# A recurrence and a gated feed-forward on one core: output copies of two superblocks on ScalarE, and another written-out order of the later steps

## The chip, the cores and the metric

The kernel runs on one core of a Trainium2 chip. A core has five engines, each with its own queue of instructions that it works off in order: PE (TensorE, matmuls; PEld is its weight load), DVE (VectorE), ACT (ScalarE), POOL (GpSimd) and SP (SyncE, which here only issues DMAs). They wait for each other by semaphores. The metric is the device time of one execution in microseconds (us); the median of several runs counts.

## The reference

Inputs r, k, v, w are float32 of shape (4 batches, 8 heads, 768 tokens, 48); u is (8, 48). For every batch and head a 48x48 state is carried along the tokens, and its output feeds a gated feed-forward over the 8 x 48 = 384 channels:

```python
for t in range(S):
    cur = einsum('bhd,bhe->bhde', u * k[t], v[t])
    y[t] = einsum('bhd,bhde->bhe', r[t], state + cur)
    state = w[t][..., None] * state + einsum('bhd,bhe->bhde', k[t], v[t])
x = y.transpose(0, 2, 1, 3).reshape(3072, 384)
xn = x / sqrt(mean(x * x, -1) + 1e-6) * rms_g
g, val = xn @ w_gate, xn @ w_val          # 384 -> 1536
out = (g * sigmoid(g) * val) @ w_out      # 1536 -> 384, float32
```

## The kernel before

The 768 tokens are cut into six superblocks n = 0..5 of 128 tokens; a superblock holds the same 128 tokens of the four batches j = 0..3, so 512 rows. A step is written name.n.j. Within a superblock the recurrence is done in chunk form, per (n, j):

- load_w, load_k, load_r, load_v (L208 to L237) bring 128 x 384 float32 each, all issued on SP. Eight buffers hold r, k and v each, and four pairs hold w.
- ln (ACT) takes logarithms of w; cs_mm (PE) makes cumulated sums in the PSUM pools ps_a and ps_b; for n of 3 to 5 cs_add (DVE) derives the second sum from the first; exp_r and exp_k (ACT) exponentiate in place, so exp_r comes after cs_add has read.
- r_mul and k_mul (DVE) scale r and k; w_tot (DVE) keeps the total decay. rk_tr transposes both, by PE and ACT (with rk_pe) for n below 2, by a DMA transpose issued on SP from n = 2 on.
- q_mm (PE) makes the 128x128 score blocks in two ps_q banks; q_mask_e (DVE, L465) copies the even heads with the mask; q_copy_o (ACT, L469) copies the odd ones, which q_mask_o (POOL, L476) then masks. q_mm.4.2 does j = 2 and 3 at once.
- st_mm (PE) makes the update of the state from k and cast_v's bf16 v (POOL from n = 2 on), st_new (DVE) applies it; y_mm (PE) makes the output of the recurrence.
- bonus_mul (POOL, two multiplications, L423 and L424, needs r and k), bonus_sum (DVE), bonus_v (POOL, needs v) make the term with u; x_add (DVE) adds it.
- x_sq (ACT), x_rstd (POOL, L524 and L525) and xn_mul (ACT) normalize; xn_pe (PE) with xn_out (DVE), or for n of 4 and 5 a DMA transpose xn_tr with xn_gain (DVE), bring xn to the layout of the feed-forward.

The feed-forward of a superblock runs over 12 units f of 128 of the 1536 channels: gate_mm and val_mm (PE, L566, three matmuls of 128x512 each, into ps_a and ps_b with two banks each), silu (ACT, L198), h_mul (DVE, L584). Then o_mm (PE, L629, twelve matmuls of 128x384) makes the output of 128 rows in a ps_q bank, o_out (L636 on DVE or L638 on ACT) copies it to one of three buffers ob, and out_dma (SP, L644) stores it. The pool ps_q has four banks for rk_pe, q_mm, st_mm, y_mm, xn_pe and o_mm together, so each of these on PE waits until the bank used four allocations earlier has been read.

Logarithm and exponential are in one ACT table, silu in another; every change of table is a load (L196) in ACT's queue. It falls ten times.

The order of everything is written out by hand in one string, ORDER (L25 to L126): the loop at its end (L647 to L650) calls the steps one by one, and each engine gets its instructions in just this order. The feed-forward of superblock n is woven with the recurrence of n + 1, and o_mm of n with the start of n + 2. What sets time is therefore where a step stands in each queue. OUT_DVE (L190) lists the (n, j) whose output copy goes to DVE; all others go to ACT.

Of the kernel before, what the change touches and what calls it, by code (L numbers as in the profile page):

```python
# [680 lines left out]
```

## Time and profile before

| what | value |
|---|---|
| median of 5 runs | 209.52 us (207.79 to 214.32) |
| profiled execution: its time, its span | 208.85 us, 207.1 us |
| PE, DVE, ACT, POOL busy | 190.2, 159.5, 138.7, 108.3 us |
| HBM read, written | 25.96 MB, 4.72 MB |
| output copies on DVE (L636), ACT (L638), full size | 12 of 554 ns, 11 of 480 ns |
| silu (L198), h_mul (L584) | 72 of 598 ns, 72 of 688 ns |
| one 128x384 load, issue to landing | 3.8 to 4.2 us (median by tensor) |

A page of the profile has the busy time of each engine, the span in 40 slices (each digit tenths of a slice), the groups of instructions with their busy time, the mean of one, and the idle time ahead of them. "A <- B: 0.8, 2, 0.4" in a list of waits means that A stood idle for B: 0.8 us in total, twice, 0.4 at the longest. In a timeline a line has the start, the duration, the engine, the line of the code, and in brackets the idle time ahead of it with what ended it. Busy time of PE counts matmuls in the pipeline.

### The profile page before, as it was taken

To read this page: it belongs to the slowest core of one execution; us is meant where nothing else is said; L and a number is where in the kernel's file an instruction comes from. 1 tells how busy PE (TensorE), PEld (TensorE's weight loads), DVE (VectorE), ACT (ScalarE), POOL (GpSimd) and SP (SyncE) were. 2 spreads that over 40 slices of the span, in tenths; PEclk is the share of its full clock that TensorE was granted. 3 is DMA by queue.
4 is the path that set the end of the run, shared out by engine and by line. 5 is a ranking of instruction groups with operands and counts; after the bars stand their busy time and mean duration, and the time that the engine had idled before them with its cause. 6 is when DMAs were issued, how large, how long until landed. Compare 5 with 4: busy or idle time off the path is not lost.

```text
span 207.1 us, 4352 instructions
## 1 busy us (share of the span) xinstructions
PE 190.2 (92%) x1507; PEld 111.7 (54%) x1524; DVE 159.5 (77%) x323; ACT 138.7 (67%) x282; POOL 108.3 (52%) x167
## 2 busy tenths in 40 slices
PE   5685869899999999998999999999999999999993
...
DMA  6999999999999899899899989997157110201032
GB/s 133 211 200 199 185 201 201 198 174 227 184 199 233 163 194 220 167 234 198 172 203 205 233 174 216 149 231 169 39 145 211 41 38 3 76 0 40 0 119 76
DMA packets 125727, 32.41 MB, mean 156 GB/s; under 512 B 120580, under 2 KB 124552, under 8 KB 125704
## 3 DMA queue, kind: packets, MB, share of 16 engines
...
HBM read 25.96 MB, written 4.72 MB: 148 GB/s over the span
## 4 chain that ended last, share of the span: by engine, by line
PE 52%; SPq 20%; POOL 8%; DMA 8%; ACT 4%; issue 4%; DVE 2%; POOLq 0%; DVEq 0%; ACTq 0%
SPq L211 16%; PE ps_a L566 16%; PE ps_b L566 15%; PE ps_q L629 14%; DMA rt<-in_r_dram 5%; SPq L228 4%; DMA wt<-in_w_dram 3%; POOL ruk L423 2%; POOL ruk L424 2%; PE ps_q L458 2%; PE ps_q L503 1%; POOL qts L476 1%; POOL ydiag L433 1%; PE ps_q L506 1%; PE ps_a L378 1%
## 5 line engine op out<-in xcount | busy, mean ns | idle before, releaser
L198 ACT ACTIVATE sg<-ps_a 128x512 bf16<-128x512 f32 x72 | 42.9, 598 | 32.0 <-PE ps_a L566 30.2
L584 DVE TENSOR_TENSOR ht<-ps_b,sg 128x512 bf16<-128x512 f32 x72 | 49.0, 688 | 19.3 <-PE ps_b L566 12.9
L566 PE MATMUL ps_a<-xnt,wg_sb 128*128 128x512 bf16 x207 | 58.6, 382 | 1.8 <-DMA wg_sb<-in_moe_w_gate_dram 1.0
L566 PE MATMUL ps_b<-xnt,wv_sb 128*128 128x512 bf16 x208 | 58.2, 382 | 0.3
L629 PE MATMUL ps_q<-wo_sb,ht 128*128 128x384 bf16 (+1 forms) x300 | 50.1, 319 | 0.0
L629 PEld LDWEIGHTS <-ht 128*128 128x128 bf16 x300 | 27.9, 98 | 16.5 <-DMA wo_sb<-in_moe_w_out_dram 0.2
L423 POOL TENSOR_TENSOR ruk<-rt,kt 128x384 f32<-128x384 f32 x24 | 24.6, 1024 | 23.1 <-DMA rt<-in_r_dram 17.4
L566 PEld LDWEIGHTS <-wv_sb 128*128 128x128 bf16 x216 | 23.6, 115 | 20.5 <-issue 1.5
L566 PEld LDWEIGHTS <-wg_sb 128*128 128x128 bf16 x216 | 23.2, 114 | 20.9 <-issue 1.2
L424 POOL TENSOR_TENSOR ruk<-ruk,u_bc 128x384 f32<-128x384 f32 x24 | 24.0, 999 | 1.9
L476 POOL TENSOR_SCALAR_AFFINE_SELECT qts<-qts 128x512 bf16<-128x512 bf16 x20 | 12.7, 634 | 14.3 <-ACT qts L469 14.3
L433 POOL TENSOR_TENSOR ydiag<-vt,diag 128x384 f32<-128x384 f32 x24 | 19.8, 829 | 0.4 <-DVE diag L428 0.4
L465 DVE TENSOR_TENSOR qts<-ps_q,mask_lt 128x512 bf16<-128x512 f32 x24 | 16.4, 683 | 2.4 <-PE ps_q L460 2.0
L529 ACT ACTIVATE xn<-xb,rstd 128x384 bf16<-128x384 f32 x24 | 14.4, 609 | 2.1 <-POOL rstd L525 1.9
L198 ACT ACTIVATE lw<-wt 128x384 bf16<-128x384 f32 x24 | 12.1, 517 | 5.1 <-DMA wt<-in_w_dram 5.0
L469 ACT CAST qts<-ps_q 128x512 bf16<-128x512 f32 x20 | 11.7, 583 | 4.5 <-PE ps_q L460 4.5
L511 DVE TENSOR_TENSOR xb<-ps_q,ydiag 128x384 f32<-128x384 f32 x24 | 13.2, 552 | 1.8 <-POOL ruk L424 0.9
L636 DVE COPY ob<-ps_q 128x384 f32<-128x384 f32 (+1 forms) x13 | 7.0, 539 | 9.3 <-PE ps_q L629 8.5
L196 ACT ACT_TABLE_LOAD x10 | 12.8, 1283 | 1.8 <-PEq L665 1.6
L516 ACT ACTIVATE junk<-xb 128x384 bf16<-128x384 f32 x24 | 12.4, 519 | 1.6 <-DVE xb L511 1.2
L417 DVE TENSOR_TENSOR rk<-kt,ps_b 128x384 bf16<-128x384 f32 x20 | 11.0, 549 | 2.5 <-ACT ps_b L198 2.2
L428 DVE TENSOR_REDUCE diag<-ruk 128x8 f32<-128x384 f32 x24 | 12.9, 543 | 0.0
...
## 6 DMA issues: line engine op xcount, KB each, us to landing
...
```

Source lines behind the costliest of these rows:

```text
L198: return nc.scalar.activation(**kw).ins
L211: dmas["load_" + which, n, j] = nc.sync.dma_start(out=inp[which, n, j], in_=t[j, :, n * L:(n + 1) * L, :].rearrange("h t d -> t h d")).ins
L423: nc.gpsimd.tensor_tensor(out=ruk[n, j], in0=inp["r", n, j], in1=inp["k", n, j], op=ALU.mult)
L424: nc.gpsimd.tensor_tensor(out=ruk[n, j], in0=ruk[n, j], in1=u_bc, op=ALU.mult)
L433: nc.gpsimd.tensor_tensor(out=ydiag[n, j], in0=inp["v", n, j], in1=diag[n, j].to_broadcast([128, H, D]), op=ALU.mult)
L465: nc.vector.tensor_tensor(out=qts[n, j][:, 0], in0=bank["q", n, j][0], in1=bc_mid(mask_lt, NP), op=ALU.mult)
L476: nc.gpsimd.affine_select(out=qts[n, j][:, 1], in_=qts[n, j][:, 1], compare_op=ALU.is_gt, fill=0.0, base=0, pattern=[[0, NP], [1, 128]], c ...
L511: nc.vector.tensor_tensor(out=xb[n, j], in0=bank.pop(("y", n, j)), in1=ydiag[n, j].rearrange("p h d -> p (h d)"), op=ALU.add)
L529: nc.scalar.activation(out=xn, in_=xb[n, j], func=AF.Copy, scale=rstd[n, j][:, 1:2])
L566: nc.tensor.matmul(ps, lhsT=units(ws, c, f), rhs=xnt[n][:, c, :], start=(c == 0), stop=(c == KC - 1))
L584: nc.vector.tensor_tensor(out=ht[n][:, f, :], in0=bank.pop(("v", n, f)), in1=bank.pop(("sg", n, f)), op=ALU.mult)
L629: nc.tensor.matmul(ps[:, cols], lhsT=ht[n][:, f, b * L:(b + 1) * L], rhs=wo_sb[:, f, cols], start=(f == 0), stop=(f == FC - 1))
```

## The change

Two edits. OUT_DVE loses 20, 22, 30 and 32: the output copies o_out.2.0, o_out.2.2, o_out.3.0 and o_out.3.2 go from DVE to ACT, so that all eight of superblocks 2 and 3 are on ACT. And ORDER is another permutation of the same 1063 steps from its 178th step on (its first sixteen lines are the same): of PE's 284 steps 80 stand in another place of its queue, of SP's 145 transfers 73, of POOL's 111 steps 71, of ACT's steps 150 and of DVE's 184, for these two partly because of the four copies. No step is added or left out, and no buffer count changes.

The diff, cut to the stretches that are spoken of:

```diff
--- before
+++ after
...
-load_r.1.2 silu.0.4 bonus_sum.1.0 gate_mm.0.5 bonus_mul.1.1 k_mul.1.1 q_mm.1.0 load_r.1.3 silu.0.5 val_mm.0.5
-h_mul.0.4 cast_v.1.0 load_w.2.0 q_mask_e.1.0 gate_mm.0.6 q_copy_o.1.0 load_wo.2.0 h_mul.0.5 rk_pe.1.1 load_r.2.0
-st_mm.1.0 k_mul.1.2 val_mm.0.6 load_wo.1.0 rk_tr.1.1 k_mul.1.3 gate_mm.0.7 bonus_mul.1.2 silu.0.6 r_mul.1.2 val_mm.0.7
-silu.0.7 h_mul.0.6 gate_mm.0.8 cast_v.1.1 load_w.2.1 st_new.1.0 rk_pe.1.2 bonus_v.1.0 val_mm.0.8 rk_tr.1.2 q_mm.1.1
-h_mul.0.7 q_mask_o.1.0 gate_mm.0.9 silu.0.8 r_mul.1.3 load_wo.0.0 q_copy_o.1.1 val_mm.0.9 bonus_sum.1.1 silu.0.9
-rk_pe.1.3 h_mul.0.8 bonus_v.1.1 st_mm.1.1 gate_mm.0.10 rk_tr.1.3 q_mask_e.1.1 bonus_mul.1.3 load_v.1.2 val_mm.0.10
+load_r.1.2 silu.0.4 bonus_sum.1.0 gate_mm.0.5 bonus_mul.1.1 cast_v.1.0 k_mul.1.1 val_mm.0.5 load_r.1.3 silu.0.5
+h_mul.0.4 st_mm.1.0 rk_pe.1.1 load_w.2.0 st_new.1.0 gate_mm.0.6 load_wo.2.0 load_v.1.2 val_mm.0.6 silu.0.6 h_mul.0.5
+load_wo.0.0 gate_mm.0.7 rk_tr.1.1 h_mul.0.6 q_mm.1.0 bonus_mul.1.2 r_mul.1.2 cast_v.1.1 val_mm.0.7 silu.0.7 k_mul.1.2
+gate_mm.0.8 q_copy_o.1.0 load_w.2.1 bonus_sum.1.1 val_mm.0.8 silu.0.8 h_mul.0.7 load_wo.1.0 gate_mm.0.9 q_mask_e.1.0
+q_mask_o.1.0 rk_pe.1.2 silu.0.9 r_mul.1.3 val_mm.0.9 bonus_mul.1.3 rk_tr.1.2 k_mul.1.3 q_mm.1.1 gate_mm.0.10 h_mul.0.8
+q_copy_o.1.1 rk_pe.1.3 q_mask_e.1.1 bonus_v.1.0 st_mm.1.1 load_k.2.0 val_mm.0.10 h_mul.0.9 rk_tr.1.3 q_mask_o.1.1
...
-out_dma.0.2 o_mm.1.0 bonus_mul.3.2 bonus_sum.3.1 x_sq.2.1 st_new.2.3 load_k.4.0 ln.3.1 xn_mul.2.0 out_dma.0.3
-cs_mm.3.0 x_add.2.2 cs_mm.3.1 ln.3.2 x_rstd.2.1 y_mm.2.3 cs_add.3.0 x_sq.2.2 o_mm.1.1 o_out.1.0 exp_k.3.0 x_rstd.2.2
-cs_add.3.1 exp_r.3.0 out_dma.1.0 k_mul.3.0 exp_k.3.1 load_r.4.0 bonus_v.2.3 r_mul.3.0 exp_r.3.1 xn_mul.2.1 xn_pe.2.0
-k_mul.3.1 bonus_mul.3.3 o_mm.1.2 rk_tr.3.0 x_add.2.3 xn_mul.2.2 r_mul.3.1 ln.3.3 o_out.1.1 xn_out.2.0 rk_tr.3.1
-x_sq.2.3 w_tot.3.0 w_tot.3.1 xn_pe.2.1 cs_mm.3.2 o_out.1.2 x_rstd.2.3 xn_pe.2.2 cs_mm.3.3 cs_add.3.2 load_k.4.1
-o_mm.1.3 xn_out.2.1 bonus_v.3.0 exp_r.3.2 load_v.3.1 cs_add.3.3 xn_mul.2.3 cast_v.3.0 xn_out.2.2 load_w.4.0 exp_r.3.3
-w_tot.3.2 exp_k.3.2 r_mul.3.2 xn_pe.2.3 q_mm.3.0 o_out.1.3 xn_out.2.3 load_k.4.2 exp_k.3.3 st_mm.3.0 k_mul.3.2
+o_mm.1.0 bonus_v.2.3 xn_mul.2.0 load_r.4.0 x_add.2.1 q_mask_o.2.3 ln.3.1 out_dma.0.3 x_add.2.2 x_sq.2.1 cs_mm.3.0
+bonus_sum.3.1 cs_mm.3.1 ln.3.2 load_k.4.0 x_rstd.2.1 o_mm.1.1 cs_add.3.0 x_sq.2.2 cs_add.3.1 exp_r.3.0 load_k.4.1
+bonus_mul.3.3 o_out.1.0 exp_k.3.0 r_mul.3.0 exp_r.3.1 k_mul.3.0 xn_mul.2.1 y_mm.2.3 xn_pe.2.0 r_mul.3.1 o_out.1.1
+o_mm.1.2 rk_tr.3.0 exp_k.3.1 x_add.2.3 x_rstd.2.2 ln.3.3 k_mul.3.1 x_sq.2.3 out_dma.1.0 xn_out.2.0 xn_mul.2.2
+x_rstd.2.3 w_tot.3.0 load_v.3.1 w_tot.3.1 xn_pe.2.1 cs_mm.3.2 o_out.1.2 cs_mm.3.3 bonus_mul.4.0 xn_pe.2.2 xn_out.2.1
+xn_mul.2.3 rk_tr.3.1 o_mm.1.3 cs_add.3.2 xn_out.2.2 exp_r.3.2 load_r.4.1 cs_add.3.3 exp_k.3.2 r_mul.3.2 load_r.4.2
+cast_v.3.0 xn_pe.2.3 q_mm.3.0 o_out.1.3 w_tot.3.2 bonus_v.3.0 xn_out.2.3 exp_r.3.3 st_mm.3.0 k_mul.3.2 load_v.3.2
+exp_k.3.3 gate_mm.2.0 r_mul.3.3 q_copy_o.3.0 val_mm.2.0 w_tot.3.3 load_v.3.3 k_mul.3.3 silu.2.0 gate_mm.2.1
...
-bonus_v.3.2 h_mul.2.7 gate_mm.2.9 bonus_sum.4.1 out_dma.1.1 q_mm.3.2 cast_v.3.3 silu.2.9 h_mul.2.8 val_mm.2.9
-bonus_mul.4.3 x_sq.3.0 load_k.5.0 q_mask_e.3.2 gate_mm.2.10 h_mul.2.9 val_mm.2.10 load_w.4.2 silu.2.10 bonus_sum.4.2
-gate_mm.2.11 out_dma.1.2 q_copy_o.3.2 bonus_v.3.3 h_mul.2.10 st_mm.3.3 val_mm.2.11 load_w.4.3 silu.2.11 q_mask_o.3.2
-st_new.3.3 ln.4.0 y_mm.3.1 x_rstd.3.0 out_dma.1.3 q_mm.3.3 load_r.5.1 h_mul.2.11 y_mm.3.2 bonus_v.4.0 x_add.3.1 ln.4.1
-cs_mm.4.0 bonus_v.4.1 q_mask_e.3.3 q_copy_o.3.3 o_mm.2.0 cs_add.4.0 x_sq.3.1 bonus_v.4.2 x_add.3.2 exp_k.4.0
-bonus_sum.4.3 q_mask_o.3.3 x_sq.3.2 k_mul.4.0 cs_mm.4.1 x_rstd.3.1 exp_r.4.0 o_mm.2.1 ln.4.2 cs_add.4.1 bonus_mul.5.0
-xn_mul.3.0 r_mul.4.0 exp_r.4.1 o_out.2.0 rk_tr.4.0 xn_mul.3.1 r_mul.4.1 xn_pe.3.0 exp_k.4.1 y_mm.3.3 o_out.2.1
-o_mm.2.2 k_mul.4.1 out_dma.2.0 x_rstd.3.2 x_add.3.3 rk_tr.4.1 xn_out.3.0 x_sq.3.3 w_tot.4.0 w_tot.4.1 xn_mul.3.2
-x_rstd.3.3 cs_mm.4.2 load_v.4.3 o_out.2.2 xn_pe.3.1 xn_pe.3.2 o_mm.2.3 load_k.5.1 cs_add.4.2 cast_v.4.0 xn_mul.3.3
-xn_out.3.1 exp_r.4.2 load_k.5.2 xn_out.3.2 exp_k.4.2 ln.4.3 r_mul.4.2 load_r.5.2 xn_pe.3.3 k_mul.4.2 cs_mm.4.3
-o_out.2.3 q_mm.4.0 xn_out.3.3 st_mm.4.0 load_k.5.3 w_tot.4.2 q_copy_o.4.0 cs_add.4.3 gate_mm.3.0 q_mask_e.4.0
-q_mask_o.4.0 exp_r.4.3 load_r.5.3 val_mm.3.0 exp_k.4.3 bonus_sum.5.0 bonus_mul.5.1 silu.3.0 q_mm.4.1 r_mul.4.3
+silu.2.7 st_mm.3.2 bonus_sum.4.0 gate_mm.2.8 st_new.3.2 load_w.4.1 bonus_mul.4.3 val_mm.2.8 silu.2.8 y_mm.3.0
+out_dma.1.3 h_mul.2.7 gate_mm.2.9 load_w.4.2 h_mul.2.8 q_mm.3.2 silu.2.9 bonus_v.3.1 val_mm.2.9 bonus_sum.4.1
+load_k.5.1 q_copy_o.3.2 q_mask_e.3.2 cast_v.3.3 gate_mm.2.10 load_r.5.1 x_add.3.0 bonus_v.3.2 val_mm.2.10 silu.2.10
+load_v.4.0 h_mul.2.9 q_mask_o.3.2 gate_mm.2.11 x_sq.3.0 h_mul.2.10 load_r.5.2 bonus_mul.5.0 st_mm.3.3 val_mm.2.11
+silu.2.11 st_new.3.3 ln.4.0 load_w.4.3 y_mm.3.1 y_mm.3.2 h_mul.2.11 q_mm.3.3 x_rstd.3.0 x_add.3.1 ln.4.1 cs_mm.4.0
+bonus_v.3.3 x_sq.3.1 o_mm.2.0 cs_add.4.0 x_add.3.2 x_rstd.3.1 exp_r.4.0 q_mask_e.3.3 q_copy_o.3.3 ln.4.2 bonus_sum.4.2
+q_mask_o.3.3 cs_mm.4.1 x_sq.3.2 o_mm.2.1 cs_add.4.1 exp_k.4.0 x_rstd.3.2 w_tot.4.0 r_mul.4.0 xn_mul.3.0 k_mul.4.0
+exp_r.4.1 bonus_mul.5.1 o_out.2.0 bonus_sum.4.3 rk_tr.4.0 xn_pe.3.0 xn_mul.3.1 y_mm.3.3 r_mul.4.1 cs_mm.4.2 exp_k.4.1
+x_add.3.3 o_mm.2.2 xn_mul.3.2 out_dma.2.0 k_mul.4.1 bonus_v.4.0 o_out.2.1 cs_add.4.2 rk_tr.4.1 x_sq.3.3 xn_out.3.0
+exp_k.4.2 x_rstd.3.3 bonus_sum.5.0 xn_pe.3.1 exp_r.4.2 xn_pe.3.2 o_mm.2.3 xn_out.3.1 load_k.5.2 cast_v.4.0 xn_mul.3.3
+r_mul.4.2 load_v.4.1 o_out.2.2 w_tot.4.1 xn_out.3.2 ln.4.3 load_r.5.3 k_mul.4.2 xn_pe.3.3 w_tot.4.2 cs_mm.4.3
+o_out.2.3 xn_out.3.3 q_mm.4.0 load_k.5.3 st_mm.4.0 cs_add.4.3 q_copy_o.4.0 gate_mm.3.0 q_mask_e.4.0 out_dma.2.1
+exp_k.4.3 q_mask_o.4.0 val_mm.3.0 exp_r.4.3 silu.3.0 bonus_mul.5.2 q_mm.4.1 load_v.4.2 r_mul.4.3 y_mm.4.0 w_tot.4.3
...
-val_mm.3.3 h_mul.3.2 silu.3.3 bonus_mul.5.3 gate_mm.3.4 x_sq.4.0 h_mul.3.3 load_v.5.1 val_mm.3.4 silu.3.4 load_v.5.2
-st_mm.4.1 gate_mm.3.5 h_mul.3.4 x_rstd.4.0 out_dma.2.2 val_mm.3.5 st_new.4.1 silu.3.5 cast_v.4.2 load_v.5.3
-gate_mm.3.6 xn_mul.4.0 q_mask_o.4.1 h_mul.3.5 val_mm.3.6 cast_v.4.3 load_w.5.0 silu.3.6 bonus_sum.5.1 bonus_v.4.3
-gate_mm.3.7 load_w.5.1 q_mask_e.4.1 val_mm.3.7 bonus_sum.5.2 load_w.5.2 q_mm.4.2 h_mul.3.6 xn_tr.4.0 gate_mm.3.8
-q_copy_o.4.2 q_mask_e.4.2 val_mm.3.8 silu.3.7 q_mask_o.4.2 q_copy_o.4.3 out_dma.2.3 y_mm.4.1 h_mul.3.7 silu.3.8
-y_mm.4.2 load_w.5.3 x_add.4.1 gate_mm.3.9 x_add.4.2 x_sq.4.1 val_mm.3.9 h_mul.3.8 x_sq.4.2 x_rstd.4.1 gate_mm.3.10
-q_mask_e.4.3 silu.3.9 x_rstd.4.2 val_mm.3.10 xn_mul.4.1 h_mul.3.9 silu.3.10 gate_mm.3.11 xn_tr.4.1 q_mask_o.4.3
-bonus_sum.5.3 h_mul.3.10 val_mm.3.11 cast_v.5.0 silu.3.11 cast_v.5.1 st_mm.4.2 xn_mul.4.2 y_mm.4.3 h_mul.3.11
-bonus_v.5.0 st_mm.4.3 ln.5.0 xn_tr.4.2 x_add.4.3 o_mm.3.0 cast_v.5.2 st_new.4.2 x_sq.4.3 st_new.4.3 ln.5.1 x_rstd.4.3
-cs_mm.5.0 ln.5.2 cs_mm.5.1 o_mm.3.1 cs_add.5.0 cast_v.5.3 xn_mul.4.3 cs_add.5.1 bonus_v.5.1 exp_r.5.0 xn_tr.4.3
-exp_k.5.0 r_mul.5.0 bonus_v.5.2 exp_k.5.1 k_mul.5.0 ln.5.3 cs_mm.5.2 o_mm.3.2 exp_r.5.1 rk_tr.5.0 cs_add.5.2 k_mul.5.1
-exp_r.5.2 r_mul.5.1 exp_k.5.2 r_mul.5.2 rk_tr.5.1 cs_mm.5.3 o_out.3.1 o_out.3.0 o_mm.3.3 cs_add.5.3 xn_gain.4.0
-out_dma.3.0 exp_k.5.3 xn_gain.4.1 xn_gain.4.2 exp_r.5.3 k_mul.5.2 gate_mm.4.0 r_mul.5.3 rk_tr.5.2 o_out.3.2 val_mm.4.0
-silu.4.0 k_mul.5.3 gate_mm.4.1 rk_tr.5.3 q_mm.5.0 val_mm.4.1 q_mask_e.5.0 q_copy_o.5.0 out_dma.3.1 gate_mm.4.2
+load_w.5.0 h_mul.3.2 silu.3.3 gate_mm.3.4 x_rstd.4.0 q_mask_e.4.1 val_mm.3.4 load_v.5.0 h_mul.3.3 bonus_v.4.2 silu.3.4
+st_mm.4.1 xn_mul.4.0 gate_mm.3.5 load_v.5.1 bonus_mul.5.3 st_new.4.1 y_mm.4.1 silu.3.5 val_mm.3.5 load_w.5.1 x_add.4.1
+gate_mm.3.6 h_mul.3.4 out_dma.2.2 x_sq.4.1 bonus_v.4.3 q_mm.4.2 h_mul.3.5 load_w.5.2 val_mm.3.6 q_copy_o.4.2
+q_mask_e.4.2 gate_mm.3.7 q_copy_o.4.3 q_mask_e.4.3 q_mask_o.4.2 load_v.5.2 silu.3.6 val_mm.3.7 cast_v.4.2 load_v.5.3
+silu.3.7 h_mul.3.6 x_rstd.4.1 gate_mm.3.8 xn_tr.4.0 bonus_sum.5.1 val_mm.3.8 bonus_v.5.0 xn_mul.4.1 h_mul.3.7 y_mm.4.2
+silu.3.8 load_w.5.3 cast_v.4.3 gate_mm.3.9 x_add.4.2 q_mask_o.4.3 xn_tr.4.1 val_mm.3.9 h_mul.3.8 x_sq.4.2 bonus_v.5.1
+gate_mm.3.10 silu.3.9 out_dma.2.3 x_rstd.4.2 val_mm.3.10 h_mul.3.9 silu.3.10 cast_v.5.0 gate_mm.3.11 xn_mul.4.2
+h_mul.3.10 cast_v.5.1 val_mm.3.11 xn_tr.4.2 bonus_sum.5.2 silu.3.11 y_mm.4.3 ln.5.0 bonus_v.5.2 h_mul.3.11 st_mm.4.2
+st_mm.4.3 x_add.4.3 cast_v.5.2 o_mm.3.0 st_new.4.2 cast_v.5.3 x_sq.4.3 ln.5.1 x_rstd.4.3 st_new.4.3 ln.5.2 cs_mm.5.0
+o_out.3.0 cs_mm.5.1 o_mm.3.1 xn_mul.4.3 cs_add.5.0 cs_add.5.1 xn_tr.4.3 exp_r.5.0 exp_k.5.0 r_mul.5.0 ln.5.3 k_mul.5.0
+out_dma.3.0 cs_mm.5.2 exp_r.5.1 o_mm.3.2 exp_k.5.1 cs_add.5.2 rk_tr.5.0 r_mul.5.1 exp_r.5.2 k_mul.5.1 exp_k.5.2
+o_out.3.1 r_mul.5.2 rk_tr.5.1 cs_mm.5.3 o_mm.3.3 cs_add.5.3 xn_gain.4.0 exp_r.5.3 xn_gain.4.1 xn_gain.4.2 exp_k.5.3
+bonus_sum.5.3 o_out.3.2 k_mul.5.2 gate_mm.4.0 bonus_v.5.3 o_out.3.3 r_mul.5.3 rk_tr.5.2 val_mm.4.0 silu.4.0 k_mul.5.3
...
-    OUT_DVE = sel("00 02 10 12 20 22 30 32 40 42 50 52 53")
+    OUT_DVE = sel("00 02 10 12 40 42 50 52 53")
```

## The prediction

> **What bounds the kernel now.** First the page's head: busy time of each engine and the span in 40 slices.
>
> ```profile
> span 207.1 us, 4352 instructions
> PE 190.2 (92%) x1507; PEld 111.7 (54%) x1524; DVE 159.5 (77%) x323; ACT 138.7 (67%) x282; POOL 108.3 (52%) x167
> ...
> PE   5685869899999999998999999999999999999993
> ...
> DMA  6999999999999899899899989997157110201032
> ```
>
> Two things are near full: the DMA engines until about 145 us, and PE from about 30 us to the end. "Busy" alone does not say that PE is at its pace, so I read next what PE waited for from 38 us on, where the two orders part (k_mul.1.1 starts at 38.9).
>
> ```profile
> PE ps_a L378 <- ACT lw L198: 0.8, 2, 0.4
> PE ps_q L486 <- ACT ob L638: 0.5, 1, 0.5
> PE ps_q L440 <- DVE rk L412: 0.4, 1, 0.4
> PE ps_q L540 <- ACT xn L529: 0.2, 1, 0.2
> PE ps_a L378 <- DVE wcol L409: 0.2, 1, 0.2
> ```
>
> That is the whole list: 2.1 us of waits in 169 us. The chain of waits agrees: from 96 us it consists almost wholly of matmuls at 0.65 us for three of 128x512, and it ends in 9.79 us of L629. The change gives PE the same instructions, so PE is the bound, and a new order wins at most about these 2.1 us plus some issue gaps; what it can lose has no such limit.
>
> Then the places where PE does wait: the o_mm stretches, here by stage.
>
> ```profile
> 84.00:97.00 13.00, 12.10 (x111) 7.37 (x108) 11.89 (x29) 11.03 (x27) 8.55 (x14) 1.00 0.92 200
> ...
> 113.00:128.00 15.00, 14.49 (x165) 9.57 (x164) 14.12 (x34) 13.31 (x29) 10.60 (x19) 1.00 0.95 210
> ...
> 144.00:157.00 13.00, 12.56 (x102) 7.45 (x100) 11.80 (x27) 10.77 (x22) 4.12 (x8) 1.00 0.42 100
> ```
>
> (Columns: stretch, length, busy PE, PEld, DVE, ACT, POOL, clock, DMA share, GB/s.) There ACT and DVE are both near full. Last, ACT in the stretch of superblock 2's output, in its timeline:
>
> ```profile
> 114.41 0.94 ACT L198 ACTIVATE lw<-wt 128x384 bf16<-128x384 f32 x2
> ...
> 121.18 0.52 ACT L516 ACTIVATE junk<-xb 128x384 bf16<-128x384 f32 x1 [0.74 <-DVE xb L511]
> ...
> 122.74 0.62 ACT L529 ACTIVATE xn<-xb,rstd 128x384 bf16<-128x384 f32 x1 [0.43 <-POOL rstd L525]
> ...
> 125.45 0.59 ACT L469 CAST qts<-ps_q 128x512 bf16<-128x512 f32 x1 [0.29 <-PE ps_q L460]
> ...
> 126.90 1.28 ACT L196 ACT_TABLE_LOAD   x1
> ```
>
> From 114.41 to 126.90 ACT idles 0.74 + 0.43 + 0.29 = 1.46 us: that is the room for more copies.
>
> **Method.** The profiled execution took 208.85 us (span 207.1); the sum is made against it. The median of the five runs, 209.52, stands 0.67 above, and I carry the difference over to it. For a moved step I take either its slot (the time of the step now in that place of its queue) or a walk with starts read from the timelines: from one ACT start to the next, ln 0.42, x_sq 0.55, exp 0.41, xn_mul 0.51, q_copy_o 0.47, an output copy 0.38 (90.74 to 91.10, 94.93 to 95.30).
>
> **The four copies.** On DVE one takes 554 ns (L636), 0.47 to the next start; on ACT 480 ns, 0.38 to the next start. So each of two stretches loses 0.94 us of DVE and gains 0.76 us of ACT. The table loads stay ten, each at the same kind of place.
>
> *Superblock 2 (113 to 128).* Walk of ACT in the new order: ln.4.0 114.41, ln.4.1, x_sq.3.1 to 115.80; exp_r.4.0 must wait for cs_add.4.0 (116.26); q_copy_o.3.3, ln.4.2, x_sq.3.2, exp_k.4.0, xn_mul.3.0, exp_r.4.1 to 119.44; o_out.2.0 to 119.82; xn_mul.3.1, exp_k.4.1, xn_mul.3.2, o_out.2.1 to 121.63; x_sq.3.3, two exps to 123.0; xn_mul.3.3 (x_rstd.3.3 at 123.1) to 123.66; o_out.2.2 to 124.04; ln.4.3 to 124.46. PE in its new order: o_mm.2.2 starts 120.2 (o_out.2.0 has freed its bank at 119.9), xn_pe.3.2 waits about 0.2 for xn_out.3.0's bank, o_mm.2.3 122.65, cs_mm.4.3 124.75, gate_mm.3.0 125.65 against 125.56 before. exp_r.4.3 ends at 126.85, the table load follows as before (126.90). The copies fit into the idle time. Price +0.2; bounds: -0.4 (the listed wait of cs_mm.4.0 goes) and +0.8 (no idle time is usable: two copies of 0.38 in full). Near the lower middle, because only 0.46 + 0.1 of waits stay in the walk.
>
> *Superblock 3 (143 to 157).* Now xn_mul.4.2 stands before silu.3.11 and not after it (143.56 to 144.19), so the table load starts about 0.4 earlier and cs_mm.5.1's wait for ln.5.1 (0.4 of the 0.8 listed) goes. Against it o_out.3.0, 3.2 and 3.3 stand ahead of silu.4.0: ACT idles 0.24 + 1.06 there now, and three copies are 1.14; silu.4.0 (now 154.95) ends near 156.4, and gate_mm.4.2, which needs its bank, starts at 156.5. Sum -0.2, bounds -0.4 and +0.6.
>
> By a rule of the skill this would be more. The Trainium skill, Perfetto Trace Analysis, Optimizing Scalar/DVE Operations, says that work of a saturated DVE may well go to ScalarE; DVE is the fuller of the two here, and by that the estimate would be a gain of all four copies, 2 us. The row against it is PE's own list: only 0.8 us of it names anything in these stretches.
>
> **The order, queue by queue.** 80 of 284 places on PE change, 73 of 145 on SP, 71 of 111 on POOL; most steps move by one to five.
>
> *38 to 53 us.* PE there waits for r_mul.1.3, which waits for load_r.1.3; that load is in the same place. cast_v.1.0 and st_mm.1.0 come earlier, q_mm.1.0 later; h_mul.0.8 now stands behind r_mul.1.3 and k_mul.1.3 (47.0 + 2 x 0.5), so val_mm.0.10 starts at 48.9 and not 48.7. +0.1; bounds -0.4 (the listed wait of L440 goes) and +0.6 (PE waits one more triple of matmuls, 0.65). load_r.2.0 moves from 42.3 to slot 53.2 and lands near 57.4 (median 4.2); bonus_mul.2.0, now at 57.2, starts about then all the same. load_wo.0.0 comes before load_wo.1.0, same total.
>
> *84 to 97 us.* xn_mul.2.3 moves ahead of exp_r.3.2, so it no longer stands behind ACT's 1.53 us wait: PE's xn_pe.2.3 wins 0.2. o_out.1.3 comes one exp earlier: st_mm.3.0's wait of 0.5 (L486) could go. But on POOL bonus_mul.4.0 now precedes cast_v.3.0, and st_mm.3.0 stands on PE ahead of gate_mm.2.0. load_k.4.0 issues in slot 88.6 and lands at 92.5 (median 3.9); bonus_mul.4.0 92.7 to 94.8 (2.08 for its two instructions), cast_v.3.0 to 95.3, st_mm.3.0 95.35 against 95.47. -0.1; bounds -0.5 and, with the longest landing that the chain shows (6.09, rt: 94.7 instead of 92.5), +2.1.
>
> *SP, 95 to 140 us.* load_v.4.0 to 4.3 move 8 to 16 places later, load_w.4.0 twelve later, the k and r loads of superblock 5 and out_dma.1.1 to 1.3 earlier. Slots (median of wt 4.1, of vt 3.8): load_w.4.0 at 108.6 lands at 112.7, used at 114.4; load_w.4.1 at 110.7 lands at 114.8, used at 114.83; load_w.4.2 at 112.1 lands at 116.2, used at 117.1; load_v.4.1 at 122.7 lands at 126.5, cast_v.4.1 then waits little, and st_mm.4.1 is at 132.6; load_v.4.3 at 131.9 lands at 135.7, st_mm.4.3 is at 144. Cost 0, covered by gate_mm and val_mm of superblock 3; load_w.4.1 has nothing to spare, but behind it ACT has the 0.46 of exp_r.4.0's wait, and cs_mm.4.1 is at 117.2; past that each late us is one us of the walk above. bonus_mul.4.1 and 4.2 on POOL wait up to 2 us for their loads; what stands behind them (cast_v.3.1, needed at 103) has that time.
>
> *130 to 142 us.* y_mm.4.1 goes 8 places up on PE, q_mm.4.2 from 137.0 to 135.3: rk_tr.4.3 lands at 133.4, so 1.9 to spare. silu.3.6 now stands behind x_sq.4.1 and two q_copy_o: it ends at 138.1, gate_mm.3.8 needs its bank at 138.2. Cost 0, cover 0.1; if missed 0.5. The output DMAs of superblock 3 go later; the last DMAs are untouched.
>
> Sum: +0.2 - 0.2 + 0.1 - 0.1 = 0.0: 208.85 for such an execution, 209.5 as a median.
>
> **Rivals.**
> - *Nothing visible because the copies were always covered* (the title's change does nothing, the rest neither): also 209.5. Apart from the forecast only in that the lists of waits stay as they are.
> - *Slower: POOL makes PE wait.* Place: bonus_mul.4.0 ahead of cast_v.3.0, st_mm.3.0 ahead of gate_mm.2.0. For it: POOL's longest waits are for just these loads (17.4 us for rt in 5 waits, longest 8.6). Against: by slot the load is 0.2 us early. Price: landing 6.1 instead of 3.9 is 2.1 at st_mm.3.0, one SP slot later 0.6 more (1.11 for two), so +2.7, with the other terms' +0.1: 212.3. It decides (over 1%) once load_k.4.0 lands after about 94.7.
> - *Faster: the new order takes PE's waits away* and adds none: 2.1, plus half of the 1.4 us that the weight loads of L381 stand in issue at the same places: 206.7. Against it: table loads and DMA landings, which cause most of them, are not shortened.
>
> **How the numbers follow.** A measurement of this kernel can tell about 1% (2.1 us) from no change. Chances: forecast 0.48, covered copies 0.10, slower rival 0.26, faster rival 0.16. Of the forecast's own spread (bounds -1.7 and +4.1 summed, hardly all at once) I give 0.03 to slower. So faster 0.16, same 0.55, slower 0.29. The forecast alone spans 208.3 to 211.3; the range takes in the faster rival, and the slower one with all but its tail: 206.7 to 213.0.
>
> **What would show it.** Right: PE busy per stage as above within 0.3 us, L636 nine instructions and L638 sixteen (now 13 and 12), ten table loads, and ACT's idle from ln.4.0 to the table load down to about 0.7. Wrong: a wait of PE L486 for POOL L339 near 95 us; PE waiting for silu's bank at gate_mm.3.8; SP standing at a transpose with loads queued behind it; or PE busy per stage falling by over a microsecond anywhere after 38 us.

## The result, and the profile after

| | before | after |
|---|---|---|
| median | 209.62 us (207.79 to 214.32, 47 runs) | 210.54 us (208.64 to 213.52, 28 runs) |
| profiled execution: its time, its span | 208.85 us, 207.1 us | 211.71 us, 210.0 us |

The ratio is 1.0057, with a 95% interval of 1.0036 to 1.0078: the change costs 0.57%, about 1.2 us. The ratio isn't the quotient of the two medians, because here and below it leaves out the executions that took over 1.5% more than the fastest of the same kernel. The forecast was 209.5 and no change.

The profiled execution of after lies 1.2 us above its own median, and part of that lies ahead of the change: the step gate_mm.0.4, which stands before the first step that differs, starts at 38.99 us in it and at 37.21 us in before (by the starts of the weight loads in PE's timeline). So 1.78 us of the 2.9 us between the two spans are scatter of the first loads: PE stood 1.26 us until 38.58 for r_mul.1.0. (In the other traces of the new order or its head gate_mm.0.4 starts anywhere from 36.62 to 40.37.) I therefore read all places from gate_mm.0.4 on.

The page of after, its head and slices (the same lines as shown of before):

```profile
span 210.0 us, 4368 instructions
...
PE 190.1 (91%) x1507; PEld 112.0 (53%) x1524; DVE 159.1 (76%) x319; ACT 139.5 (66%) x286; POOL 109.4 (52%) x167
...
PE   5685859795999999999999899999999999999993
...
DMA  6998999989977999999999859998555120110032
```

PE is as busy as before (190.1 us for 190.2), in a longer span: PE has lost time by waiting. The slices say where: the tenth slice (47.3 to 52.5 us) has 5, where before had 9. (The eighth, 36.8 to 42, has 7 for 8, but it holds the wait until 38.58, which lies ahead of the change.) What PE waited for from 38 us on:

```profile
PE ps_q L440 <- DVE rk L412: 2.6, 2, 1.4
PE ps_q L440 <- DVE rk L417: 0.9, 1, 0.9
PE ps_a L378 <- ACT lw L198: 0.6, 1, 0.6
PE ps_a L378 <- DVE rk L412: 0.4, 1, 0.4
PE ps_q L503 <- DVE qts L465: 0.2, 1, 0.2
```

The two waits for ob and for xn are gone; new is a wait of 0.9 of the transposes (L440) for k_mul (L417), which before's list doesn't have. Of the 2.6 for r_mul (L412), 1.26 are the wait until 38.58; the other, which compares with before's 0.4, is 1.37. Both new waits belong to superblock 1, at 50 to 52.5 us. The stages of the copies, about 3 us later than before, in the table by stretch:

```profile
38.00:53.00 15.00, 11.99 (x93) 6.86 (x96) 13.02 (x21) 8.17 (x14) 11.76 (x12) 1.00 1.01 190
...
87.00:100.00 13.00, 12.82 (x138) 8.45 (x137) 12.77 (x32) 11.69 (x28) 10.19 (x16) 1.00 1.01 209
116.00:131.00 15.00, 14.38 (x165) 9.64 (x165) 13.87 (x33) 13.95 (x31) 10.65 (x19) 1.00 0.79 170
147.00:160.00 13.00, 12.51 (x95) 7.34 (x94) 11.42 (x26) 11.33 (x24) 3.15 (x7) 1.00 0.57 119
```

PE's first number in the two lower lines is 14.38 and 12.51, against 14.49 and 12.56 before: the copies changed nothing there. Work has gone from DVE (14.12 to 13.87, 11.80 to 11.42) to ACT (13.31 to 13.95, 10.77 to 11.33). In the first line PE is 11.99 (12.54 if the window is shifted by the 1.78 us, to 39.78:54.78); in before's own line for this stretch it is 14.34:

```profile
38.00:53.00 15.00, 14.34 (x133) 8.24 (x134) 12.90 (x25) 11.16 (x18) 11.04 (x13) 1.00 1.05 197
```

ACT beside superblock 2's output, in its timeline of after (only the lines with idle time, the two moved copies at 122.16 and 126.40, and the table load):

```profile
119.04 0.48 ACT L198 ACTIVATE ps_a<-ps_a 128x388 f32<-128x388 f32 x1 [0.22 <-DVE ps_b L389]
...
122.16 0.48 ACT L638 COPY ob<-ps_q 128x384 f32<-128x384 f32 x1
...
125.88 0.61 ACT L529 ACTIVATE xn<-xb,rstd 128x384 bf16<-128x384 f32 x1 [0.18 <-POOL rstd L525]
126.40 0.46 ACT L638 COPY ob<-ps_q 128x384 f32<-128x384 f32 x1
...
127.64 0.48 ACT L638 COPY ob<-ps_q 128x384 f32<-128x384 f32 x1 [0.35 <-ACT lw L198]
128.36 0.59 ACT L469 CAST qts<-ps_q 128x512 bf16<-128x512 f32 x1 [0.24 <-PE ps_q L460]
...
129.73 1.28 ACT L196 ACT_TABLE_LOAD   x1
```

The idle time from ln.4.0 to the table load is 0.22 + 0.18 + 0.35 + 0.24 = 0.99 us (1.46 before), and the table load follows PE as before.

The distances between PE's milestones say the same in one table (us, from the starts of the weight loads):

| from, to | before | after |
|---|---|---|
| gate_mm.0.4, o_mm.0.0 | 16.18 | 18.34 |
| o_mm.0.0, o_mm.1.0 | 30.48 | 30.40 |
| o_mm.1.0, gate_mm.2.0 | 11.74 | 10.84 |
| gate_mm.2.0, o_mm.2.0 | 19.61 | 19.60 |
| o_mm.2.0, gate_mm.3.0 (superblock 2's copies) | 10.24 | 10.20 |
| gate_mm.3.0, o_mm.3.0 | 18.73 | 18.68 |
| o_mm.3.0, gate_mm.4.0 (superblock 3's copies) | 9.35 | 9.36 |
| gate_mm.4.0, o_mm.5.4 | 49.09 | 49.09 |

The head loses 2.16, one stretch gives 0.90 back, everything else is 0.0 to 0.1. Together 1.1 us, which is about what the ratio says; but that the sum fits is luck. The 2.16 hold 1.0 us of longer waiting for r_mul (1.37 for 0.4) that is scatter of the loads: in five other traces with this order of loads PE waits 0 to 0.5 for it (order alone, bonus_mul late, the two with one group of copies back, only k_mul.1.3 moved, all below). And the 0.90 is no gain of the new order, as the account of the prediction shows at the end.

### The profile page after: what moved, and what is told of

It reads as the page before. It is cut to its first block, busy times and chain, and to the rows that moved or that the text cites. A ratio compares the mean times of both kernels' runs of the same rounds, so it can differ in the third digit from the quotient of the medians.

```text
span 210.0 us, 4368 instructions
## 1 busy us (share of the span) xinstructions
PE 190.1 (91%) x1507; PEld 112.0 (53%) x1524; DVE 159.1 (76%) x319; ACT 139.5 (66%) x286; POOL 109.4 (52%) x167
## 4 chain that ended last, share of the span: by engine, by line
PE 64%; SPq 19%; DVE 5%; DMA 4%; issue 2%; POOL 2%; ACT 2%; ACTq 0%; POOLq 0%; DVEq 0%
PE ps_q L629 19%; PE ps_a L566 18%; PE ps_b L566 18%; SPq L211 15%; DMA rt<-in_r_dram 4%; SPq L228 3%; PE ps_q L458 2%; PE ps_q L503 1%; PE ps_q L506 1%; PE ps_a L378 1%; PE ps_q L486 1%; PE ps_q L540 1%; DVE xb L511 1%; POOL ydiag L433 1%; ACT L196 1%
## 5 line engine op out<-in xcount | busy, mean ns | idle before, releaser
L584 DVE TENSOR_TENSOR ht<-ps_b,sg 128x512 bf16<-128x512 f32 x72 | 48.5, 687 | 20.1 <-PE ps_b L566 12.8
L423 POOL TENSOR_TENSOR ruk<-rt,kt 128x384 f32<-128x384 f32 x24 | 25.2, 1050 | 30.6 <-DMA rt<-in_r_dram 26.6
L629 PEld LDWEIGHTS <-ht 128*128 128x128 bf16 x300 | 28.0, 98 | 16.3
L424 POOL TENSOR_TENSOR ruk<-ruk,u_bc 128x384 f32<-128x384 f32 x24 | 24.5, 1023 | 1.9
L465 DVE TENSOR_TENSOR qts<-ps_q,mask_lt 128x512 bf16<-128x512 f32 x24 | 16.3, 683 | 1.8 <-PE ps_q L460 1.4
L476 POOL TENSOR_SCALAR_AFFINE_SELECT qts<-qts 128x512 bf16<-128x512 bf16 x20 | 12.6, 635 | 9.4 <-ACT qts L469 9.3
L638 ACT COPY ob<-ps_q 128x384 f32<-128x384 f32 (+1 forms) x16 | 7.5, 467 | 9.8 <-PE ps_q L629 9.4
L412 DVE TENSOR_TENSOR rk<-rt,ps_a 128x384 bf16<-128x384 f32 x20 | 11.0, 548 | 2.1 <-DMA rt<-in_r_dram 1.4
```

Of the source, the lines that this page charges most:

```text
L423: nc.gpsimd.tensor_tensor(out=ruk[n, j], in0=inp["r", n, j], in1=inp["k", n, j], op=ALU.mult)
L424: nc.gpsimd.tensor_tensor(out=ruk[n, j], in0=ruk[n, j], in1=u_bc, op=ALU.mult)
L465: nc.vector.tensor_tensor(out=qts[n, j][:, 0], in0=bank["q", n, j][0], in1=bc_mid(mask_lt, NP), op=ALU.mult)
L584: nc.vector.tensor_tensor(out=ht[n][:, f, :], in0=bank.pop(("v", n, f)), in1=bank.pop(("sg", n, f)), op=ALU.mult)
L629: nc.tensor.matmul(ps[:, cols], lhsT=ht[n][:, f, b * L:(b + 1) * L], rhs=wo_sb[:, f, cols], start=(f == 0), stop=(f == FC - 1))
```

## Where the head's time goes

Superblock 1 is the only one whose exponentials are left in SBUF, as er and ek; for superblocks 0 and 2 to 5 they are in PSUM (ps_a, ps_b). The groups of instructions of before, which part r_mul (L412) and k_mul (L417) by that:

```profile
L417 DVE TENSOR_TENSOR rk<-kt,ps_b 128x384 bf16<-128x384 f32 x20 | 11.0, 549 | 2.5 <-ACT ps_b L198 2.2
L412 DVE TENSOR_TENSOR rk<-rt,ps_a 128x384 bf16<-128x384 f32 x20 | 10.8, 548 | 2.0 <-DMA rt<-in_r_dram 1.9
L412 DVE TENSOR_TENSOR rk<-rt,er 128x384 bf16<-128x384 f32 x4 | 3.0, 754 | 1.8 <-DMA rt<-in_r_dram 1.8
L417 DVE TENSOR_TENSOR rk<-kt,ek 128x384 bf16<-128x384 f32 x4 | 2.2, 554 | 1.0 <-DMA kt<-in_k_dram 0.9
```

And the same two groups of after:

```profile
L417 DVE TENSOR_TENSOR rk<-kt,ek 128x384 bf16<-128x384 f32 x4 | 4.1, 1037 | 0.0
L412 DVE TENSOR_TENSOR rk<-rt,er 128x384 bf16<-128x384 f32 x4 | 2.9, 725 | 4.3 <-DMA rt<-in_r_dram 4.3
```

The same instruction on the same number of bytes: 554 ns became 1037 (mean of four), while the forms with one operand in PSUM take 548 or 549. The four are 0.55, 0.89, 1.36 and 1.35 us; DVE's timeline in after shows the two longest (k_mul.1.2 and k_mul.1.3), and POOL's what ran beside them. DVE:

```profile
45.22 0.55 DVE L412 TENSOR_TENSOR rk<-rt,er 128x384 bf16<-128x384 f32 x1
45.69 1.36 DVE L417 TENSOR_TENSOR rk<-kt,ek 128x384 bf16<-128x384 f32 x1
...
50.60 0.56 DVE L412 TENSOR_TENSOR rk<-rt,er 128x384 bf16<-128x384 f32 x1 [1.90 <-DMA rt<-in_r_dram]
51.08 1.35 DVE L417 TENSOR_TENSOR rk<-kt,ek 128x384 bf16<-128x384 f32 x1
```

POOL (L423 and L424 are the two instructions of bonus_mul):

```profile
45.29 1.34 POOL L423 TENSOR_TENSOR ruk<-rt,kt 128x384 f32<-128x384 f32 x1 [1.18 <-DMA rt<-in_r_dram]
46.71 1.19 POOL L424 TENSOR_TENSOR ruk<-ruk,u_bc 128x384 f32<-128x384 f32 x1
...
50.74 1.27 POOL L423 TENSOR_TENSOR ruk<-rt,kt 128x384 f32<-128x384 f32 x1 [1.64 <-DMA rt<-in_r_dram]
52.09 1.20 POOL L424 TENSOR_TENSOR ruk<-ruk,u_bc 128x384 f32<-128x384 f32 x1
```

And PE, which needs k_mul for the second half of the transposes (rk_pe.1.3):

```profile
51.22 0.40 PE L440 MATMUL ps_q<-ident,rk 128*128 128x128 bf16 x4 [1.37 <-DVE rk L412]
52.48 0.40 PE L440 MATMUL ps_q<-ident,rk 128*128 128x128 bf16 x4 [0.87 <-DVE rk L417]
```

With 0.56 us k_mul.1.3 would have ended at 51.64, just as the first half of the transposes does (51.62). So by this estimate nearly the whole wait of 0.87 is the lengthening of k_mul, 0.79.

The landing of r releases two engines at once: r_mul on DVE and bonus_mul on POOL. In the new order k_mul.1.2 and k_mul.1.3 stand directly behind r_mul.1.2 and r_mul.1.3, so each starts about 0.4 us after bonus_mul's start (45.69 against 45.29, 51.08 against 50.74), and ends only 0.41 or 0.42 us after bonus_mul's first instruction has ended (47.05 against 46.63, 52.43 against 52.01). In before, both k_mul ran ahead of r_mul, as soon as k was there, when POOL did not compute (it issued two weight transfers, L319):

```profile
41.75 1.17 DVE L417 TENSOR_TENSOR rk<-kt,ek 128x384 bf16<-128x384 f32 x2 [0.45 <-DMA kt<-in_k_dram]
...
46.97 0.57 DVE L412 TENSOR_TENSOR rk<-rt,er 128x384 bf16<-128x384 f32 x1 [0.60 <-DMA rt<-in_r_dram]
```

That gives the theory: the loss is the two k_mul that meet POOL, and the place of k_mul in ORDER makes it. The Trainium skill, SBUF — State Buffer, Who interferes with whom, says that a DVE instruction with two SBUF inputs contends with a GpSimd instruction that reads SBUF, that this contention is an exclusive lock, and that a DVE instruction with at most one SBUF input, outside the modes that use both of its port pairs, does not contend. The rows agree: 1.35 instead of 0.56 for kt and ek, a mean of 548 or 549 ns with an operand in PSUM.

The rivals were: the copies themselves cost time; the loads in another order land r later (the wait for L412); the tail of the order; that a k_mul behind r_mul is late whether it meets POOL or not; and that the loss is simply PE's wait at rk_pe.1.3 and nothing else.

## The experiments

All were timed in five rounds against before on the same chip. There are three sets on three chips (before's medians are 209.12, 207.33 and 207.89), so the ratios are to be compared and not the times; all ratios are to before, with 95% intervals. The letters of the theories are those of the expectations.

**The copies alone.** The old order, with the new OUT_DVE:

```diff
-    OUT_DVE = sel("00 02 10 12 20 22 30 32 40 42 50 52 53")
+    OUT_DVE = sel("00 02 10 12 40 42 50 52 53")
```

> The order of before, with only the four output copies moved to ACT. Theory A (the loss comes from the new order of the steps between 38 and 57 us, around rk_pe.1.3, and the copies are covered): within 0.3% of before. Theory B (the copies on ACT are the cost): the whole loss, some +0.6% or 1.2 us, and PE later by that much between o_mm.2.0 and gate_mm.4.0.

Measured: 209.7 against 209.12, ratio 1.0035 (1.0004 to 1.0066). In the trace o_mm.2.0 to gate_mm.3.0 takes 10.62, not 10.24, and o_mm.3.0 to gate_mm.4.0 9.35 as before. In the old order the copies win nothing; they are a small loss, if anything.

**The order alone.** The new ORDER, with the old OUT_DVE (the diff above the other way round).

> The new order, with the four copies left on DVE. Theory A: the whole loss stays, about +0.6%. Theory B: the loss goes, within 0.2% of before.

Measured: 212.83 against 209.12, ratio 1.0177 (1.0139 to 1.0216), three times the loss of the whole change, which neither theory had foreseen. PE's waits from 140 to 160 us:

```profile
PE ps_a L378 <- DVE rk L412: 1.0, 1, 1.0
PE ps_b L566 <- DVE rk L417: 0.2, 1, 0.2
```

In after the first of them is 0.4 and the second isn't there, and o_mm.3.0 to gate_mm.4.0 takes 9.94 instead of 9.36. So the two edits belong together: the new order needs DVE to be free of the copies.

**Which part of the order.** Two kernels split ORDER at o_mm.0.0, between 53 and 57 us. The first has the new kernel's steps up to there, and behind it the old order and the old copies (70 of its 1063 steps stand in another place than in before). The second has the old steps up to there, the new ones behind, and the new copies.

```diff
-gate_mm.0.5 bonus_mul.1.1 k_mul.1.1 q_mm.1.0 load_r.1.3 silu.0.5
+gate_mm.0.5 bonus_mul.1.1 cast_v.1.0 k_mul.1.1 val_mm.0.5 load_r.1.3 silu.0.5
...
-bonus_sum.1.2 x_sq.1.0 q_mask_o.1.2 o_mm.0.0 load_k.2.1
+bonus_sum.1.2 x_sq.1.0 q_mask_o.1.2 load_r.2.0 o_mm.0.0 load_k.2.1
```

> The 256 steps that stand ahead of o_mm.0.0 in both orders run in the new order, all later ones in the old order, copies as in before. Theory A: the head alone costs about 2.0 us (as in the traces: PE 1.8 late before the change begins, 3.9 late at o_mm.0.0), so +0.9%, more than the whole change, because the later part of the new order gave back 1.1 us. Theory C (the head's 2 us in the one trace is only scatter of the loads, and the loss is spread over the later stages): within 0.3% of before.

> The same 256 steps in the old order, all later ones in the new order, with the four copies on ACT. Theory A: the tail gains the 1.1 us that the traces show between o_mm.0.0 and gate_mm.2.0, so -0.5%. Theory C: the loss is here, +0.6%.

Measured: the new head alone 211.16, ratio 1.0075 (1.0041 to 1.0109); the old head with the new tail 209.64, ratio 1.0022 (0.9989 to 1.0055). The new head alone loses as much as the whole change or more; the old head with the new tail can't be told from before. That the new tail gains half a per cent (A) is not confirmed.

**k_mul to its old place.** The kernel after, with k_mul.1.2 and k_mul.1.3 moved up, in front of r_mul.1.2; nothing else changes.

```diff
-val_mm.0.6 silu.0.6 h_mul.0.5 load_wo.0.0 gate_mm.0.7 rk_tr.1.1 h_mul.0.6 q_mm.1.0
+val_mm.0.6 silu.0.6 h_mul.0.5 k_mul.1.2 k_mul.1.3 load_wo.0.0 gate_mm.0.7 rk_tr.1.1 h_mul.0.6 q_mm.1.0
...
-bonus_mul.1.2 r_mul.1.2 cast_v.1.1 val_mm.0.7 silu.0.7 k_mul.1.2 gate_mm.0.8
+bonus_mul.1.2 r_mul.1.2 cast_v.1.1 val_mm.0.7 silu.0.7 gate_mm.0.8
...
-val_mm.0.9 bonus_mul.1.3 rk_tr.1.2 k_mul.1.3 q_mm.1.1
+val_mm.0.9 bonus_mul.1.3 rk_tr.1.2 q_mm.1.1
```

> The new kernel, with k_mul.1.2 and k_mul.1.3 on DVE back ahead of r_mul.1.2, right after h_mul.0.5. Theory D (the loss of the head comes from k_mul.1.2 and 1.3 standing behind r_mul, where POOL's bonus_mul starts at the same moment on the same landing of r, so that a k_mul takes 1.35 us instead of 0.56 and rk_pe.1.3 waits for it): k_mul 0.56 to 0.9 us, no wait of L440 for L417, st_mm.1.1 within 0.5 us of the start of rk_pe.1.3; the time falls by 0.8 to 1.2 us, to +0.1% of before. Theory E (the loss comes from the order of the loads): no change, +0.6%.

Measured: 207.79 against 207.33, ratio 0.9998 (0.9969 to 1.0028). The loss is gone. DVE in its timeline:

```profile
42.02 1.02 DVE L417 TENSOR_TENSOR rk<-kt,ek 128x384 bf16<-128x384 f32 x2
...
45.89 1.88 DVE L412 TENSOR_TENSOR rk<-rt,er 128x384 bf16<-128x384 f32 x1
```

Both k_mul together take 1.02. But r_mul.1.3 now takes 1.88: it meets two POOL instructions one after the other. PE stands only 0.4 for it, as it did in before, so a long multiply is not paid for everywhere.

**k_mul late in the old kernel.** The reverse: before, with k_mul.1.2 put behind r_mul.1.2 and k_mul.1.3 behind r_mul.1.3.

```diff
-st_mm.1.0 k_mul.1.2 val_mm.0.6 load_wo.1.0 rk_tr.1.1 k_mul.1.3 gate_mm.0.7 bonus_mul.1.2 silu.0.6 r_mul.1.2 val_mm.0.7
+st_mm.1.0 val_mm.0.6 load_wo.1.0 rk_tr.1.1 gate_mm.0.7 bonus_mul.1.2 silu.0.6 r_mul.1.2 k_mul.1.2 val_mm.0.7
...
-h_mul.0.7 q_mask_o.1.0 gate_mm.0.9 silu.0.8 r_mul.1.3 load_wo.0.0
+h_mul.0.7 q_mask_o.1.0 gate_mm.0.9 silu.0.8 r_mul.1.3 k_mul.1.3 load_wo.0.0
```

> The kernel before, with k_mul.1.2 right behind r_mul.1.2 and k_mul.1.3 right behind r_mul.1.3, nothing else moved. bonus_mul.1.3 here stands behind bonus_v.1.1 on POOL, so only k_mul.1.2 surely meets a bonus_mul. Theory D: k_mul.1.2 takes about 1.35 us, k_mul.1.3 up to that where POOL works beside it; PE waits 0.6 to 1.2 us more at rk_pe.1.3; +0.3% to +0.6%. Theory E: within 0.2% of before.

Measured: 208.55 against 207.33, ratio 1.0049 (1.0021 to 1.0077): the loss of the whole change (0.57%) from these two moves alone. The trace has one meeting, k_mul.1.2 at 43.71, and PE waits for it; k_mul.1.3, also directly behind its r_mul, meets no multiply:

```profile
43.71 1.35 DVE L417 TENSOR_TENSOR rk<-kt,ek 128x384 bf16<-128x384 f32 x1
...
48.00 0.55 DVE L417 TENSOR_TENSOR rk<-kt,ek 128x384 bf16<-128x384 f32 x1
```

```profile
PE ps_q L440 <- DVE rk L417: 0.9, 1, 0.9
```

POOL's L423 ran from 43.35 to 44.65 there, so k_mul ended 0.41 us behind it again. And the second k_mul is the test of the rival that its place alone is the cost: it takes 0.55, and PE's eight transposes of rk_pe.1.3 run without a pause:

```profile
48.31 0.69 PE L440 MATMUL ps_q<-ident,rk 128*128 128x128 bf16 x8
```

The place costs PE a wait only where it leads to a meeting.

**The loads.** The kernel after, with its loads from load_w.2.0 to load_k.2.1 in the old sequence:

```diff
-gate_mm.0.6 load_wo.2.0 load_v.1.2 val_mm.0.6 silu.0.6 h_mul.0.5 load_wo.0.0 gate_mm.0.7
+gate_mm.0.6 load_wo.2.0 load_r.2.0 val_mm.0.6 silu.0.6 h_mul.0.5 load_wo.1.0 gate_mm.0.7
...
-st_mm.1.1 load_k.2.0 val_mm.0.10
+st_mm.1.1 load_v.1.2 val_mm.0.10
...
-o_mm.0.0 load_r.2.0 bonus_sum.1.3
+o_mm.0.0 load_k.2.1 bonus_sum.1.3
```

> The new kernel, with its twelve transfers from load_w.2.0 to load_k.2.1 (load_wo among them) in the sequence of the kernel before, in the places that they have in the new one. Theory D: the k_mul stay at 1.35 us and the loss stays, +0.6%. Theory E: the loss of the head goes, to within 0.2% of before.

Measured: 209.16 against 207.33, ratio 1.0076 (1.0043 to 1.0108). The loss stays, and so do the meetings (the three latest k_mul take 559, 1344 and 1355 ns). The order of the loads is not the cause.

**bonus_mul out of the way.** The kernel after, with bonus_mul.1.3 behind bonus_v.1.1, so that k_mul.1.3 should be alone:

```diff
-r_mul.1.3 val_mm.0.9 bonus_mul.1.3 rk_tr.1.2 k_mul.1.3 q_mm.1.1
+r_mul.1.3 val_mm.0.9 rk_tr.1.2 k_mul.1.3 q_mm.1.1
...
-st_new.1.1 gate_mm.0.11 silu.0.10 bonus_v.1.1 y_mm.1.0
+st_new.1.1 gate_mm.0.11 silu.0.10 bonus_v.1.1 bonus_mul.1.3 y_mm.1.0
```

> The new kernel, with only bonus_mul.1.3 moved on POOL from ahead of bonus_v.1.0 to behind bonus_v.1.1, so that POOL does not multiply while k_mul.1.3 runs. Theory D: k_mul.1.3 takes 0.56 us if POOL idles then, and up to 1.35 if bonus_v or the mask meets it; with 0.56 us st_mm.1.1 comes 0.8 us earlier and the time falls by about 0.4%, to +0.2% of before. If k_mul.1.3 shortens and the time does not, then the wait at rk_pe.1.3 is made up for later and the head's loss lies elsewhere. Theory E: no change.

Measured: 208.11 against 207.33, ratio 1.0034 (1.0008 to 1.0059): between before and after, but not clear of after (1.0036 to 1.0078). k_mul.1.3 was not alone: it took 0.98 (47.91 to 48.89) beside POOL's masking L476 (47.69 to 48.49). PE's wait for it fell from 0.9 to 0.5, by as much as k_mul became shorter. That the time follows in proportion is not shown.

**Both edits.** The kernel after, with k_mul early (as above) and bonus_mul.1.3 late (as above).

> The new kernel with k_mul.1.2 and 1.3 early and, besides, bonus_mul.1.3 behind bonus_v.1.1 on POOL. With only the first of the two, r_mul.1.3 itself took 1.87 us beside POOL. Theory D: r_mul.1.3 shortens towards 0.6 us unless bonus_v meets it in turn; up to 0.6 us less than before, so between -0.3% and 0. Theory F (POOL has work there whatever its order, so something of it always meets r_mul.1.3): within 0.2% of before, as with the k_mul alone.

Measured: 208.9 against 207.89, ratio 1.0058 (1.003 to 1.0087): a miss. Neither edit's gain is left. The three latest r_mul by duration (minimum, median, maximum in ns):

```profile
L412 DVE TENSOR_TENSOR rk<-rt,er x3: 559/1355/1692, 37.7 to 47.2; 128x384 bf16<-128x384 f32 x3
```

The meetings have moved from k_mul to r_mul (F), whatever POOL instruction stands there. That does not explain all: with the same 16.33 us from gate_mm.0.4 to o_mm.0.0 as a good order, the trace loses 0.4 at st_mm.1.3 (0.23 of it a wait for cast_v, L337) and 0.7 more at xn_pe.1.2 (a wait of 0.73 for xn_mul), between 58 and 63 us, measured against after. The trace with k_mul early alone loses 0.5 at xn_pe.1.2 as well. Why is not settled.

**One group of copies back.** The kernel after, with superblock 3's two copies on DVE, and one with superblock 2's:

```diff
-    OUT_DVE = sel("00 02 10 12 40 42 50 52 53")
+    OUT_DVE = sel("00 02 10 12 30 32 40 42 50 52 53")
```

> The new kernel with the copies o_out.3.0 and o_out.3.2 back on DVE, those of superblock 2 on ACT. The new order with all four on DVE took 1.2% more than with all four on ACT. Theory G (it is superblock 3's boundary, where cs_mm.5.2 waits 0.6 us longer for r_mul.5.0, that stands behind o_out.3.0 on DVE): +0.3% against the new kernel, so +0.9% against before. Theory H (it is superblock 2's boundary): as the new kernel, +0.6%.

```diff
-    OUT_DVE = sel("00 02 10 12 40 42 50 52 53")
+    OUT_DVE = sel("00 02 10 12 20 22 40 42 50 52 53")
```

> The new kernel with the copies o_out.2.0 and o_out.2.2 back on DVE, those of superblock 3 on ACT. Theory G: within 0.2% of the new kernel, so about +0.6% against before. Theory H: up to +1.7% against before, and PE later between o_mm.2.0 and gate_mm.3.0.

Measured: 210.36 and 209.91 against 207.89, ratios 1.0111 (1.0071 to 1.0151) and 1.0088 (1.0055 to 1.0122). Against the change's 1.0057 that is some 0.5% and 0.3%, together two thirds of the 1.2% that the order alone lost more; the 0.3% is not clear of noise by the times. For superblock 3 the place is visible (G): o_mm.3.0 to gate_mm.4.0 takes 9.94 again, as it did with the order alone, and gate_mm.4.0 to o_mm.5.4 takes 49.46 in both, for 49.09. In DVE's timeline a copy stands ahead of cs_add (L389):

```profile
148.35 0.56 DVE L636 COPY ob<-ps_q 128x384 f32<-128x384 f32 x1
148.94 1.03 DVE L389 TENSOR_TENSOR ps_b<-ps_a,lw 128x384 f32<-128x384 f32 x2
150.05 0.56 DVE L412 TENSOR_TENSOR rk<-rt,ps_a 128x384 bf16<-128x384 f32 x1
```

From o_mm.3.0 (144.98 here, 147.05 in after) to the first cs_add it is 3.96 us; in after, where that cs_add starts at 150.42, it is 3.37. So the copy pushes cs_add back by 0.59, and with it the exps, r_mul and, at L378, PE. For superblock 2 the boundary is 10.45 (10.20 in after), and 18.89 (18.68) in the stretch behind.

**Only k_mul.1.3 moved.** The kernel after, with k_mul.1.3 directly behind k_mul.1.2, away from rk_pe.1.3 but still behind r_mul.1.2:

```diff
-r_mul.1.2 cast_v.1.1 val_mm.0.7 silu.0.7 k_mul.1.2 gate_mm.0.8
+r_mul.1.2 cast_v.1.1 val_mm.0.7 silu.0.7 k_mul.1.2 k_mul.1.3 gate_mm.0.8
...
-val_mm.0.9 bonus_mul.1.3 rk_tr.1.2 k_mul.1.3 q_mm.1.1
+val_mm.0.9 bonus_mul.1.3 rk_tr.1.2 q_mm.1.1
```

> The new kernel with only k_mul.1.3 moved, from behind r_mul.1.3 to right behind k_mul.1.2, which stays behind r_mul.1.2. Theory D, if the wait that counts is rk_pe.1.3's: k_mul.1.2 still takes 1.35 us, PE no longer waits for L417 at rk_pe.1.3, and the time falls as with both moved, to within 0.2% of before. If k_mul.1.2 counts as much: half of the gain, +0.3%.

Measured: 209.79 against 207.89, ratio 1.0062 (1.0025 to 1.0099): the whole loss is still there, so D in its narrow form (the wait at rk_pe.1.3 is the loss) has failed. DVE:

```profile
43.73 2.63 DVE L417 TENSOR_TENSOR rk<-kt,ek 128x384 bf16<-128x384 f32 x2
46.28 0.54 DVE L428 TENSOR_REDUCE diag<-ruk 128x8 f32<-128x384 f32 x1
46.74 0.68 DVE L584 TENSOR_TENSOR ht<-ps_b,sg 128x512 bf16<-128x512 f32 x1
```

PE's waits:

```profile
PE ps_b L566 <- DVE ht L584: 1.9, 1, 1.9
```

Now both k_mul meet bonus_mul.1.2, one with each of its instructions, and together take 2.63 us. PE no longer waits for L417 at all; it waits 1.9 for the h_mul (L584) that stands behind them. So the loss is what DVE loses ahead of whatever PE needs next, about 0.8 us a meeting (1.35 less 0.56), and not one particular wait; where PE doesn't need DVE soon, as at r_mul.1.3 with k_mul early, it is not paid.

The stretch of the head over the traces: from gate_mm.0.4 to o_mm.0.0 the kernels with k_mul ahead of r_mul took 16.18 (before), 16.27 (copies alone), 15.63 (k_mul early), 16.33 (both edits) and 17.25 (old head, in which 0.7 is a wait for a weight DMA), mean 16.3. Those with k_mul behind took 18.34 (after), 16.98 (order alone), 17.28 (k_mul late), 17.21 (old loads), 17.13 (bonus_mul late), 18.09 and 16.31 (one group of copies back) and 17.38 (k_mul.1.3 moved), mean 17.3; the new head alone is left out, as its traced execution took 2.4 us more than its median. The difference of 1.0 us is about that of the ratios. Single traces scatter by as much: one of the eight shows no loss here, though its k_mul are just as long, so no one trace could have settled this. PE's waits part the two groups more sharply: in seven of the eight PE waits 0.5 to 0.9 for a k_mul, and in the eighth 1.9 for the h_mul behind it; in the five it never waits for a k_mul there.

## Why the prediction was wrong, step by step

- **38 to 53 us, +0.1 with an upper end of +0.6: this step failed.** It measured about +1.0 (means of the traces); the whole change is 1.2 by the ratio. The prediction saw that r_mul.1.3 and k_mul.1.3 are now neighbours, but costed both at 0.5 and looked only for who stands behind them (h_mul.0.8), not for what runs on POOL at the same time. Its upper end was one triple of matmuls, worked out from PE's pace, not from DVE's. The row that would have told it was in before's groups: r_mul with er 754 ns, k_mul with ek 554, both with PSUM operands 548. One r_mul, at 33.88, already took 1.33 beside POOL's L424 (33.80 to 34.80). With that as the bound of each moved k_mul, two meetings of 0.8 give +1.6 at most, and the measured +1.0 lies within it.
- **What PE waits for there.** The prediction said that PE waits for r_mul.1.3 and that its load keeps its place. True, and a wait for L412 is still in the list (the 1.37); but rk_pe.1.3 also needs k_mul.1.3, which before had been done 4 us earlier (42.9) and now came last.
- **Superblock 2's boundary, +0.2: measured 0.0** (10.24 to 10.20). The walk along ACT was right in kind: the copies fit into idle time, which went from 1.46 to 0.99 (0.7 expected), and the table load comes in the same place. But the wait of cs_mm.4.0 for ln, which was to go, grew from 0.4 to 0.6.
- **Superblock 3's boundary, -0.2: measured 0.0** (9.35 to 9.36). The wait of 0.4 for ln did go, but one of 0.4 for r_mul came (L378 for L412): the bank that PE writes next is freed later.
- **The rule that offloading a saturated DVE may pay**, which the prediction weighed (the Trainium skill, Perfetto Trace Analysis, Optimizing Scalar/DVE Operations), with an estimate of 2 us: in the old order it does not hold (1.0035). In the new order the copies are worth 1.0177 less 1.0057, some 1.2% or 2.5 us. Both come from the same four instructions; whether an offload pays is a matter of what stands behind them in DVE's queue.
- **84 to 97 us, -0.1: about 0.** The stretch took 0.90 less in after than in before, but that is before's own scatter: o_mm.1.0 to gate_mm.2.0 takes 11.74 in before, and 10.63 and 10.64 in two other kernels with the old order there (copies alone; k_mul late), where after has 10.84, and three other kernels with the new order there have 11.21 to 11.79 (old head; k_mul early; order alone). So the waits that before's list has there (L486 for ob, L540 for xn) come and go from one execution to the next: in the lists of copies alone and k_mul late they are missing. No run shows that they were something to win.
- **Loads from 95 to 140, and 130 to 142: 0, as forecast** (19.60 and 18.68 against 19.61 and 18.73).
- **The rivals.** The slower one had the right engine and the wrong mechanism: POOL did make PE wait, through DVE, at 45 to 52 us, and not with a late cast_v.3.0; no wait of L486 for L339 is in the list of after. The faster one did not occur. In its list of wrong signs the prediction had named PE busy falling by over a microsecond in a stage: 14.34 to 11.99 in the first stretch is that, and 12.54 if the window is shifted as above.

Open: why the two edits together are no better than none, though no k_mul is long in them; how the loss divides between k_mul.1.2 and k_mul.1.3; whether the new tail gains anything (its interval is 0.9989 to 1.0055). No version tried was faster than both kernels; the best, the kernel after with k_mul early, is level with before.
